# Weight pieces converted in pairs, in place at stride 2, in an attention + SwiGLU kernel on Trainium2

## The chip, the cores and the metric

The kernel runs on one core of one Trainium2 chip. The metric is the time of one execution on the device in microseconds (us); the median of three runs of the kernel before is 1545.31 us. Five engines work side by side and are tied together by semaphores: TensorE (PE, with its weight loads PEld), VectorE (DVE), ScalarE (ACT), GpSimd (POOL) and SyncE (SP, which issues nearly all DMAs). [...]

## The reference, cut to what matters

The inputs arrive as follows: q, k and v have 8 sequences x 12 heads x 448 positions x 64, and the three weight matrices (768 x 1536, 768 x 1536, 1536 x 768) hold 64-bit floats, because they are scaled by a 64-bit number. TensorE multiplies 32-bit floats, so the kernel has to convert the weights on the chip.

```python
q_n, k_n = rmsnorm(q, g_q), rmsnorm(k, g_k)
attn = softmax(q_n @ k_n.T / sqrt(64))        # per sequence and head
x = (attn @ v) -> rows of 768 (12 heads x 64), 3584 rows
xn = rmsnorm(x, rms_g)
g = xn @ w_gate
out = (g * sigmoid(g) * (xn @ w_val)) @ w_out
```

## The kernel before, in words

The work of `safe_scores` goes by pairs of heads, g = 0 to 47, six for each sequence. A pair's attention is a run of score and value products on TensorE with exponentials on ScalarE between them (`score`, `rests`, `values` and `sums` for the first six pairs; `step` and `totals` later). Two halves of each pair's keys and queries are transposed on TensorE by `turn(g, 0)` and `turn(g, 1)`; both write a PSUM tile "tr", and VectorE copies out kT (L550, L552), while ScalarE copies out qT (L549). GpSimd makes the norms of q and k (L514, L515, L520), adds up the exponentials (`es`, L709 and L714), and for two pairs in each sequence scales the last 64 rows (`rest`, L465 to L469).

The first six pairs (g = 0 to 5) and most of the seventh run alone, since there is no x yet to feed the second block. From g = 7 on, the feed-forward work of the previous sequence is cut into items in the list `todo`, and `fill` places some of them between the attention parts of a pair. For the first sequence these are 48 items of `plain` (L1440: six matrix instructions each, 2.25 us), and then 12 items of `project_out` (L1178). From the second sequence on the products use a scheme with fewer multiplications on sums of weight blocks (L1081, L1305, L1373).

All order is written out by hand: `pe(fn)` issues a piece of TensorE work and counts time by one, and `after(n, fn)` puts off work of other engines by n such counts.

The weights come in 72 pieces of 128 x 384 elements: 48 of the gate and value matrices, used by the 48 items of `plain` in that order, and 24 of the output matrix. `convert` is called once per conversion turn (not to be confused with `turn`, the transposes) and handles several pieces at different stages. In conversion turn n it

- adds the two parts of piece n - 5 on GpSimd (L890) into a block of the pool `free_w`, which has NW = 23 blocks;
- joins piece n - 4 on VectorE (`join`, L848 to L850): clamp, shift and mask, and put in sign and exponent bit;
- splits piece n - 3 on ScalarE (`split`, L842 and L843): the absolute value of the high words into a tile `top`, and the scaled low words in place, at a stride of two words, in the raw tile;
- loads piece n on SP (L829) into a raw tile of 64-bit numbers, and stores piece n - 7 in DRAM (`keep`, L878) for the later sequences.

There are 7 raw tiles and 6 tiles for `top`; some of the first 24 pieces borrow a tile of the pool "xs" for `top`. The first conversion turns run in the pairs that are alone: four in g = 0, three in g = 1, three in each of g = 2 to 5, and three in g = 6. So 22 turns are done when the items begin, and after each item `fill` calls `convert` once more, if a block is free (`room`). A block comes free one count after the item that used the piece. After the last turn the tiles of the conversion are handed over to later work, and only then may `ask` begin to load weights for the second sequence.

The lines that the prediction speaks of besides: L566 and L664 are the exponentials; L596 to L598 and L638 are the inversion of a pair's sums and its use; L643 and L644 make and add the squares of x (`rd`, `ss`); L728, L730, L738 and L744 are the root mean square of x and its use (six operations L744 per sequence, put off by 0 to 5 counts); L696 and L699 copy the sums (`rd`) out of PSUM; L1448 is the tanh, L1449 and L1451 are the two products of an item group of `plain`; L530 (`norm_k`) scales the keys, L493 and L457 square them.

Of the kernel before, what the change touches and what calls it, by code (L numbers as in the profile page):

```python
# [8 lines left out]
F32 = mybir.dt.float32  # L9
I32 = mybir.dt.int32  # L10
U32 = mybir.dt.uint32
I64 = mybir.dt.int64
ALU = mybir.AluOpType
ACT = mybir.ActivationFunctionType
# [8 lines left out]
NPAIR = H // 2  # L23
NDC, NFC = DM // 128, DF // 128
HALF = DM // 2
BW = 384
HT = S // 2
# [308 lines left out]
def safe_scores(  # L336
# [20 lines left out]
    nc = tc.nc  # L357

    def pool(name, bufs, **kw):
        return ctx.enter_context(tc.tile_pool(name=name, bufs=bufs, **kw))  # L360

    NW = 23
    const, small = pool("c_const", 1), pool("c_small", 4)
    qk_pool, v_pool, qn_pool, qkT_pool = pool("c_qk", 3), pool("c_v", 3), pool("c_qn", 1), pool("c_qkT", 2)
    e_pool, tmp, y_pool, rest_pool = pool("c_e", 11), pool("c_tmp", 1), pool("c_y", 3), pool("c_rest", 2)
    x_pool, s_pool, slots = pool("c_x", 4), pool("c_xs", 3), pool("c_slots", 1)
    raw_pool, cv_pool, l2_pool = pool("c_raw", 7), pool("c_cv", 6), pool("c_l2", 5)
    scratch = pool("c_dram", 1, space=DRAM)
    ps_s, ps_m, ps_f = pool("c_ps_s", 4, space=PSUM), pool("c_ps_m", 1, space=PSUM), pool("c_ps_f", 3, space=PSUM)

# [3 lines left out]
    st = {}  # L374
# [426 lines left out]
    carried = []  # L801
    free_w = [slots.tile([128, BW], F32, name=f"w{i}") for i in range(NW)]

# [19 lines left out]
    def data(key):  # L823
        return st[key][0][:, 0:BW]

    def load_raw(src):
        raw = raw_pool.tile([128, 2 * BW], I32, name="raw")
        a = src.shape[1]
        nc.sync.dma_start(out=raw.rearrange("p (a n w) -> p a (n w)", a=a, w=2).bitcast(I64), in_=src)  # L829
        return raw  # L830

    def split(raw, n):


        words = raw.rearrange("p (n w) -> p n w", w=2)
        lo, hi = words[:, :, 0], words[:, :, 1]
        if n < 24 and n % 7 > 3:

            top = s_pool.tile([128, 3, HT], I32, name="xs")[:, 0:2].rearrange("p c n -> p (c n)")[:, 0:BW]
        else:  # L840
            top = cv_pool.tile([128, BW], I32, name="top")
        nc.scalar.activation(top.bitcast(F32), hi.bitcast(F32), ACT.Abs)  # L842
        nc.scalar.activation(lo, lo.bitcast(U32), ACT.Copy, scale=2.0**-29)  # L843
        return lo, hi, top

    def join(lo, hi, top):

        nc.vector.tensor_scalar(top.bitcast(F32), top.bitcast(F32), 122879.9921875, 2.0**-15, ALU.min, ALU.max)  # L848
        nc.vector.tensor_scalar(top, top, 3, 0x3FFFFFF8, ALU.logical_shift_left, ALU.bitwise_and)  # L849
        nc.vector.scalar_tensor_tensor(top, hi, -(2**30), top, ALU.bitwise_and, ALU.bitwise_or)  # L850
        return lo, top


    pieces = []
# [11 lines left out]
    room_so = []  # L866
# [13 lines left out]
    def convert():  # L880

        n = turn_of["n"]
        if n >= TURNS or not room(1):
            return False
        turn_of["n"] += 1
        if 0 <= n - 5 < len(pieces):
            key = pieces[n - 5][0]
            st[key] = block()
            lo, top = st.pop(("cv", n - 5))
            nc.gpsimd.tensor_tensor(data(key).bitcast(I32), top, lo, ALU.add)  # L890
        if 0 <= n - 4 < len(pieces):
            st["cv", n - 4] = join(*st.pop(("cv", n - 4)))
        if 0 <= n - 3 < len(pieces):
            st["cv", n - 3] = split(st.pop(("raw", n - 3)), n - 3)
        if n < len(pieces):
            st["raw", n] = load_raw(pieces[n][1])
        if 0 <= n - 7 < len(pieces):
            keep(pieces[n - 7][0])
        if turn_of["n"] == TURNS:

            free_w.extend(cv_pool.tile([128, BW], F32, name="top") for _ in range(4))
            whole = [raw_pool.tile([128, 2 * BW], F32, name="raw") for _ in range(7)]
            room_so.extend(whole[:6])
            homes = [whole[6][:, 0:BW], whole[6][:, BW:]] + [cv_pool.tile([128, BW], F32, name="top")[:, :] for _ in range(2)]
            carried.extend(t.rearrange("p (c n) -> p c n", c=KG) for t in homes)
        return True

# [670 lines left out]
    def turns(n):  # L1578

        for _ in range(n):  # L1580
            convert()
# [18 lines left out]
    for g in range(NG + 1):  # L1600
# [24 lines left out]
        if g <= NPAIR:  # L1625
            pe(lambda: score(g, (0,)))
            squares(g + 2, 0)
            squares(g + 2, 1)
            if g > 1:
                pe(lambda: turn(g + 1, 0))  # L1630
                some_rests(g)
                pe(lambda: turn(g + 1, 1))
            pe(lambda: rests(g))
            pe(lambda: values(g - 1))
            if g == 1:
                pe(lambda: turn(g + 1, 0))
                some_rests(g)
                pe(lambda: turn(g + 1, 1))
            load_v(g + 2)

            turns(1 if g == 1 else 3 if g < NPAIR else 0)
            pe(lambda: sums(g - 1))
            pe(lambda: score(g, (1, 2)))
            turns(2 if g == 1 else 3 if g == NPAIR else 0)
            if g == 2:
                bound()
            if g == NPAIR - 1:
                for half in range(2):
                    norm_k(g + 2, half)
            continue  # L1650
# [90 lines left out]
```

## Time and profile before

| What | Value |
|---|---|
| median of 3 runs | 1545.31 us (1544.56 to 1545.82) |
| profiled execution | 1546.19 us |
| its span in the profile | 1544.4 us |
| busy share of VectorE, ScalarE, GpSimd over the span | 60%, 35%, 48% |
| mean granted TensorE clock | 0.996 of full speed |
| last conversion turn's work on VectorE | ends near 276 us |

The profile is one execution taken by the hardware profiler. Times within it are counted from the start of the span. A group of instructions is named by line of the kernel, engine, operation, and the tiles out<-in; "x63" is how many there are. A wait is named by the instruction that waited and by what released it. A timeline row gives start, length, engine, line and, in brackets, idle time before the instruction and what ended it. The granted clock is the share of TensorE's full clock.

### The profile page before, as it was taken

The numbers are of one execution on the slowest core, as the hardware profiler recorded it, in microseconds if no ns is written. First come the engines' busy times: TensorE is split into PE (matmuls) and PEld (weight loads), VectorE is DVE, ScalarE is ACT, GpSimd is POOL, SyncE is SP. The second block draws the span as 40 slices with busy tenths as digits, with TensorE's granted clock in tenths as the row PEclk, the third lists the DMA queues.
The fourth block names the chain that finished last, engine by engine and source line by source line (L and its number), as shares of the span: only waits on it lengthen the run. The fifth ranks groups of instructions, "written<-read, shape, count | busy, mean of one in ns | idle before, by whom it ended". The sixth has DMA issues, their size and how long they took to land.

```text
span 1544.4 us, 26111 instructions
## 1 busy us (share of the span) xinstructions
PE 1511.2 (98%) x8900; PEld 1187.4 (77%) x8900; DVE 929.8 (60%) x1793; ACT 534.8 (35%) x1241; POOL 736.4 (48%) x718
## 2 busy tenths in 40 slices
PE   8999998999999999999999999999999999999997
PEld 4344444688856888888987888767987889899997
DVE  5788998667754666854457443444458444673464
ACT  6856664333323333234233332424333232101000
POOL 6868887546424354474435652544545731030003
PEclk9999999999999999999999999999999999999998
DMA  7758575776989978886557855584557755577565
GB/s 194 228 153 258 175 228 157 225 229 214 294 274 275 310 253 266 285 250 188 160 163 217 267 176 153 152 275 131 174 155 228 240 160 148 164 256 256 175 194 176
DMA packets 314082, 327.26 MB, mean 212 GB/s; under 512 B 84308, under 2 KB 310868, under 8 KB 313940
## 3 DMA queue, kind: packets, MB, share of 16 engines
q1 hardware_dynamic: 313012, 325.31, 68.1%
q8 instruction: 73, 1.20, 0.3%
q14 instruction: 69, 0.57, 0.1%
q10 hardware_dynamic: 800, 0.20, 0.1%
q0 software_dynamic: 128, 0.00, 0.0%
HBM read 271.62 MB, written 53.77 MB: 211 GB/s over the span
## 4 chain that ended last, share of the span: by engine, by line
PE 83%; DVE 11%; DMA 2%; issue 1%; ACT 1%; POOL 1%; SPq 0%; DVEq 0%; POOLq 0%; ACTq 0%
PE ff L1081 42%; PE ff L1373 10%; PE sc L659 7%; PE av L674 6%; PE ff L1305 5%; PE ff L1440 4%; PE tr L544 2%; PE ff L1178 2%; DVE top L850 1%; DVE top L849 1%; PE den L692 1%; PE den L606 1%; DVE top L848 1%; PE sc L562 1%; DVE l L1248 1%
## 5 line engine op out<-in xcount | busy, mean ns | idle before, releaser
L1081 PE MATMUL ff<-x,w 128*128 128x224 f32 x1686 | 344.4, 354 | 0.0
L1081 PEld LDWEIGHTS ff<-x,w 128*128 128x128 f32 x1686 | 315.2, 190 | 13.2 <-issue 11.3
L1081 PE MATMUL ff<-xs,w 128*128 128x224 f32 x1296 | 265.2, 353 | 2.0 <-DVE w L1003 1.2
L714 POOL TENSOR_TENSOR es<-es,e 128x448 f32<-128x448 f32 x205 | 245.9, 1200 | 13.7
L1081 PEld LDWEIGHTS ff<-xs,w 128*128 128x128 f32 x1296 | 243.9, 190 | 3.4 <-issue 1.5
L659 PE MATMUL sc<-qT,kT 64*64 64x448 f32 x1176 | 233.8, 542 | 5.7 <-ACT e L664 2.9
L674 PE MATMUL av<-e,vt 64*64 64x448 f32 x984 | 194.2, 541 | 0.0
L664 ACT ACTIVATE e<-sc 128x448 f32<-128x448 f32 x294 | 154.4, 547 | 71.4 <-PE sc L659 53.5
L644 POOL TENSOR_TENSOR ss<-ss,rd 128x448 f32<-128x448 f32 x40 | 48.0, 1201 | 218.5 <-ACT rd L643 218.5
L659 PEld LDWEIGHTS sc<-qT,kT 64*64 64x64 f32 x1176 | 79.3, 133 | 87.4 <-issue 61.6
L709 POOL TENSOR_TENSOR es<-e 128x448 f32<-128x448 f32 x41 | 48.2, 1176 | 178.0 <-ACT e L664 178.0
L515 POOL TENSOR_TENSOR rs<-ms,mhalf 128x12 f32<-128x12 f32 (+1 forms) x50 | 115.9, 2319 | 4.2
L1093 DVE TENSOR_TENSOR cc<-ff,u 128x448 f32<-128x448 f32 x84 | 52.3, 623 | 99.6 <-PE ff L1081 99.5
L1440 PE MATMUL ff<-x,w 128*128 128x448 f32 x288 | 111.8, 541 | 0.0
L674 PEld LDWEIGHTS av<-e,vt 64*64 64x64 f32 x984 | 66.2, 133 | 42.4 <-issue 42.4
L1100 ACT ACTIVATE th<-c 128x224 f32<-128x224 f32 x42 | 16.3, 389 | 238.1 <-DVE c L1093 238.1
L1373 PE MATMUL ff<-w,l 128*128 128x192 f32 x500 | 95.6, 329 | 2.8 <-DVE l L1248 2.0
L1440 PEld LDWEIGHTS ff<-x,w 128*128 128x128 f32 x288 | 53.3, 190 | 51.1 <-issue 49.2
L1373 PEld LDWEIGHTS ff<-w,l 128*128 128x128 f32 x500 | 82.6, 190 | 8.1 <-DVE l L1248 3.2
L1345 POOL TENSOR_TENSOR y<-y,c 128x384 f32<-128x384 f32 x10 | 12.2, 1217 | 159.4 <-DVE y L1414 148.0
L1093 DVE TENSOR_TENSOR u<-ff,p 128x448 f32<-128x448 f32 x42 | 26.2, 623 | 84.3 <-PE ff L1081 77.9
L1093 DVE TENSOR_TENSOR u<-ff,u 128x448 f32<-128x448 f32 x42 | 26.1, 623 | 82.6 <-PE ff L1081 82.3
(209 smaller groups left out, 2627.9 us busy)
## 6 DMA issues: line engine op xcount, KB each, us to landing
w<-kept SPq DMA_DIRECT2D x474, 192.0 KB, 3.7
w<-kept_q SPq DMA_DIRECT2D x297, 192.0 KB, 3.8
w<-kept_o SPq DMA_DIRECT2D x132, 192.0 KB, 3.9
kept<-w SPq DMA_DIRECT2D x81, 192.0 KB, 3.9
top<-kept SPq DMA_DIRECT2D x78, 192.0 KB, 3.9
top<-kept_q SPq DMA_DIRECT2D x53, 192.0 KB, 3.2
kept_q<-w SPq DMA_DIRECT2D x52, 192.0 KB, 3.0
qk<-in_q_dram SPq DMA_DIRECT2D x48, 192.0 KB, 3.5
```

What stands on the lines that cost most here:

```text
L515: nc.gpsimd.tensor_tensor(st["rs", g][:, cols], ms, mhalf[:, cols], ALU.pow)
L644: after(m, lambda: (nc.gpsimd.tensor_tensor(ss, ss, rd, ALU.add), st.update({("summed", b): hp})))
L659: nc.tensor.matmul(ps[r, 0:S], lhsT=st["kT", g][r, keys_of(i)], rhs=st["qT", g][r, :], start=True, stop=True)
L664: nc.scalar.activation(e, ps[:, 0:S], ACT.Exp)
L674: nc.tensor.matmul(st["av", g][own(j), 0:S], lhsT=vt, rhs=st["e", g, i][r], start=i == 0, stop=i == PARTS - 1, skip_group_check=True)
L709: nc.gpsimd.tensor_tensor(st["es", g], st["e", g, 0], st["e", g, 1], ALU.add)
L714: nc.gpsimd.tensor_tensor(st["es", g], st["es", g], st["e", g, i], ALU.add)
L1081: nc.tensor.matmul(bank[:, w * HT:(w + 1) * HT], lhsT=wt[:, c * 128:(c + 1) * 128], rhs=x[:, c, :], start=onto is None and w == c == 0, st ...
L1093: nc.vector.tensor_tensor(add[name], ps[:, 0:S], add[other], ALU.add)
L1305: nc.tensor.matmul(ps, lhsT=left_o(b, which, LEFT_O[name], c), rhs=data(("wo", b, name, c)), start=first and c == 0, stop=c == NFP - 1, sk ...
L1373: nc.tensor.matmul(ps, lhsT=a[:, j, :], rhs=data(key)[:, n % 2 * HW:(n % 2 + 1) * HW], start=start and j == 0, stop=j == KG - 1, skip_grou ...
L1440: nc.tensor.matmul(bank[w][:, 0:S], lhsT=data(key)[:, c * 128:(c + 1) * 128], rhs=st["x", 0, half][:, c, :], start=half == c == 0, stop=ha ...
```

## The change

Two pieces are loaded, split and joined together. A raw tile now holds two pieces (4 tiles of double size in place of 7), a tile `low` holds the scaled low words of two pieces (3 tiles of double size in place of 6 tiles `top`), and the pool "xs" is no longer borrowed. The split writes the scaled low words contiguously into `low`, and then the absolute values of the high words into the low words' places in the raw tile, which are two words apart. The join's three operations therefore read and write at a stride of two words, in place, 768 elements each instead of 384. The addition on GpSimd stays one per piece; it reads the stride-2 part from `raw` in place of the former stride-2 low words.

In time, a pair m is loaded in turn 2m, split in turn 2m + 3 (odd turns only), joined in turn 2m + 4 (even turns only), and its two pieces are added in turns 2m + 5 and 2m + 6. In each of the pairs g = 2 to 5, which run alone, four turns are made in place of three, so that 26 are done when the items begin. NW goes from 23 to 21. With 21 pieces added and none used, no block is free then: the item with index 0 is followed by no turn, and the item with index k (1 to 48) by turn 25 + k, where it was turn 22 + k before. In the items of the output product there is again no free block until the second row tile gives blocks back, so that the turns after the items with index 49, 50 and 51 fall out, and the last turns come at the same items as before.

```diff
-    NW = 23
+    NW = 21
...
-    raw_pool, cv_pool, l2_pool = pool("c_raw", 7), pool("c_cv", 6), pool("c_l2", 5)
+    raw_pool, cv_pool, l2_pool = pool("c_raw", 4), pool("c_cv", 3), pool("c_l2", 5)
...
-    def load_raw(src):
-        raw = raw_pool.tile([128, 2 * BW], I32, name="raw")
-        a = src.shape[1]
-        nc.sync.dma_start(out=raw.rearrange("p (a n w) -> p a (n w)", a=a, w=2).bitcast(I64), in_=src)
+    def load_raw(srcs):
+        raw = raw_pool.tile([128, 4 * BW], I32, name="raw")
+        for i, src in enumerate(srcs):
+            part = raw[:, i * 2 * BW:(i + 1) * 2 * BW].rearrange("p (a n w) -> p a (n w)", a=src.shape[1], w=2)
+            nc.sync.dma_start(out=part.bitcast(I64), in_=src)
         return raw

-    def split(raw, n):
+    def split(raw):
         words = raw.rearrange("p (n w) -> p n w", w=2)
         lo, hi = words[:, :, 0], words[:, :, 1]
-        if n < 24 and n % 7 > 3:
-            top = s_pool.tile([128, 3, HT], I32, name="xs")[:, 0:2].rearrange("p c n -> p (c n)")[:, 0:BW]
-        else:
-            top = cv_pool.tile([128, BW], I32, name="top")
-        nc.scalar.activation(top.bitcast(F32), hi.bitcast(F32), ACT.Abs)
-        nc.scalar.activation(lo, lo.bitcast(U32), ACT.Copy, scale=2.0**-29)
-        return lo, hi, top
-
-    def join(lo, hi, top):
+        low = cv_pool.tile([128, 2 * BW], I32, name="low")
+        nc.scalar.activation(low, lo.bitcast(U32), ACT.Copy, scale=2.0**-29)
+        nc.scalar.activation(lo.bitcast(F32), hi.bitcast(F32), ACT.Abs)
+        return lo, hi, low
+
+    def join(top, hi, low):
         nc.vector.tensor_scalar(top.bitcast(F32), top.bitcast(F32), 122879.9921875, 2.0**-15, ALU.min, ALU.max)
         nc.vector.tensor_scalar(top, top, 3, 0x3FFFFFF8, ALU.logical_shift_left, ALU.bitwise_and)
         nc.vector.scalar_tensor_tensor(top, hi, -(2**30), top, ALU.bitwise_and, ALU.bitwise_or)
-        return lo, top
+        return low, top
...
+        m, odd = divmod(n, 2)
         if 0 <= n - 5 < len(pieces):
             key = pieces[n - 5][0]
             st[key] = block()
-            lo, top = st.pop(("cv", n - 5))
-            nc.gpsimd.tensor_tensor(data(key).bitcast(I32), top, lo, ALU.add)
-        if 0 <= n - 4 < len(pieces):
-            st["cv", n - 4] = join(*st.pop(("cv", n - 4)))
-        if 0 <= n - 3 < len(pieces):
-            st["cv", n - 3] = split(st.pop(("raw", n - 3)), n - 3)
-        if n < len(pieces):
-            st["raw", n] = load_raw(pieces[n][1])
+            pair, at = divmod(n - 5, 2)
+            lo, top = st["cv", pair]
+            cols = slice(at * BW, (at + 1) * BW)
+            nc.gpsimd.tensor_tensor(data(key).bitcast(I32), top[:, cols], lo[:, cols], ALU.add)
+            if at:
+                st.pop(("cv", pair))
+        if odd and ("raw", m - 1) in st:
+            st["cv", m - 1] = split(st.pop(("raw", m - 1)))
+        if not odd and ("cv", m - 2) in st:
+            st["cv", m - 2] = join(*st["cv", m - 2])
+        if not odd and n < len(pieces):
+            st["raw", m] = load_raw([src for _, src in pieces[n:n + 2]])
...
-            turns(1 if g == 1 else 3 if g < NPAIR else 0)
+            turns(1 if g == 1 else 4 if g < NPAIR else 0)
```

The lines left out of the diff hand the four raw and three low tiles over to later work after the last turn; together with the 21 blocks they give 27 blocks again, as 23 and 4 did before.

## The prediction

> **What bounds the kernel now.** I read the page first, for the share of each engine:
>
> ```profile
> PE 1511.2 (98%) x8900; PEld 1187.4 (77%) x8900; DVE 929.8 (60%) x1793; ACT 534.8 (35%) x1241; POOL 736.4 (48%) x718
> ```
>
> TensorE is busy 98% of the span, so nothing can be gained beyond its waits. Next come the waits of TensorE in the first 330 us, the only part in which weights are converted (engine, line, what it waited for: us in total, times, longest):
>
> ```profile
> PE tr L544 <- DVE kT L550: 3.2, 1, 3.2
> PE sc L659 <- ACT e L664: 2.9, 1, 2.9
> PE sc L659 <- DVE x L744: 2.7, 1, 2.7
> ```
>
> Three waits make 8.8 us; all the other waits of that list are 1.5 us or less. In order of time they end at 199.35 us (on ACT), 240.53 (on kT) and 261.14 (on x). The busy time in stretches says which engine is late there (columns: stretch, length, then busy of PE, PEld, DVE, ACT, POOL, granted clock, DMA):
>
> ```profile
> 180.00:200.00 20.00, 17.07 (x78) 8.02 (x80) 19.52 (x31) 9.96 (x25) 18.79 (x19) 1.00 0.36 101
> ...
> 220.00:240.00 20.00, 17.36 (x103) 8.24 (x101) 19.38 (x27) 13.40 (x31) 13.72 (x13) 1.00 0.85 248
> 240.00:260.00 20.00, 17.87 (x73) 9.35 (x73) 19.52 (x34) 7.96 (x17) 14.64 (x14) 1.00 0.55 172
> 260.00:280.00 20.00, 18.86 (x80) 10.32 (x81) 9.82 (x18) 7.28 (x18) 12.62 (x12) 0.91 0.20 65
> ```
>
> VectorE is busy 97% around all three; GpSimd is nearly full around the first alone. After the third the granted clock falls (0.57 from 262 to 266 us), which is another 0.43 x 4 = 1.7 us. From 280 us on TensorE hardly waits, so what is saved before that should reach the end. The groups of VectorE up to 330 us show what fills it, and the times of the single line show why (min/median/max ns):
>
> ```profile
> L850 DVE SCALAR_TENSOR_TENSOR top<-raw,top 128x384 int32<-128x384 int32 x63 | 51.6, 818 | 2.2
> L849 DVE TENSOR_SCALAR top<-top 128x384 int32<-128x384 int32 x63 | 45.9, 728 | 2.2
> L848 DVE TENSOR_SCALAR top<-top 128x384 f32<-128x384 f32 x63 | 39.1, 621 | 4.5 <-ACT top L842 4.5
> ```
> ```profile
> L848 DVE TENSOR_SCALAR top<-top x63: 342/525/1283, 26.7 to 275.0; 128x384 f32<-128x384 f32 x63
> ```
>
> With the nine that use xs, the three operations take 603 + 708 + 803 = 2.11 us per piece on average (sums of both groups over 72). Undisturbed they take 0.342 + 0.359 + 0.557 = 1.26 us (minima of the three lines). The other 0.86 us, 0.29 per instruction, is waiting beside GpSimd: in the timeline long ones end when a GpSimd operation ends. The 240.53 wait in the timeline of VectorE, and the 199.35 one on GpSimd:
>
> ```profile
> 236.88 0.86 DVE L848 TENSOR_SCALAR top<-top 128x384 f32<-128x384 f32 x1
> 237.78 1.17 DVE L849 TENSOR_SCALAR top<-top 128x384 int32<-128x384 int32 x1
> 238.98 1.37 DVE L850 SCALAR_TENSOR_TENSOR top<-raw,top 128x384 int32<-128x384 int32 x1
> 240.27 0.21 DVE L550 COPY kT<-tr 128x64 f32<-128x64 f32 x1
> ```
> ```profile
> 193.90 1.64 POOL L466 TENSOR_TENSOR msr<-msr,mhalf 128x6 f32<-128x6 f32 x1
> 195.61 0.96 POOL L469 TENSOR_TENSOR rest<-rest,msr 128x384 f32<-128x384 f32 x1
> 196.53 6.95 POOL L890 TENSOR_TENSOR w<-top,raw 128x384 int32<-128x384 int32 x6
> ```
> ```profile
> 197.88 0.55 ACT L842 ACTIVATE top<-raw 128x384 f32<-128x384 f32 x1 [6.03 <-POOL w L890]
> ```
>
> The small kT copy stands behind three joins; the exponentials of the pair stand behind a split that waits 6.03 us for the first of six late additions, which gives its top buffer back.
>
> [...]
>
> **The change part by part.**
> *Joins.* Two pieces now cost three instructions of 768 instead of six of 384. [...] Three waits beside GpSimd instead of six: 0.86. So 2.92 us per pair of pieces against 4.23. [...] I take 2.92: the read at stride 2 and ScalarE's write were free. From the start of the interleaved part (97 us) before joins 54 pieces, 54 x 2.11 = 114 us; after joins 25 pairs, 73 us. 41 us leave an engine that had 10.5 us idle from 100 to 260.
> *Splits.* Four activations start 0.45 us apart (1.80 us). Two of 768 take 563 + 384 x 0.8 = 0.87 us each (slope from 421 ns for 256 and 523 for 384, L457), the second waiting for the first: 1.75 us. Nothing is gained, but it comes in one lump.
> *Low buffers.* Three pair buffers: a split now waits for an addition issued three turns earlier, not four. Splits fall on odd turns. The last turns of the item groups ending at 168, 193 and 220 us are odd (49, 57, 65), so there ScalarE waits one more addition (1.05) and holds 0.87 more before the exponentials: 1.9 us. At 168 the timeline shows 0.16 us of slack on the den banks and rd copies that wait for TensorE until 169.07: cost 0.8. At 199 GpSimd should be some 1 us earlier, with less waiting beside VectorE: cost 0.9. At 220 ScalarE had 1.6 us of idle time: 0.1, left out.
> *Joins before kT.* Pairs 11 and 12 have a pair join right ahead of L550. At 213.12 it ran 0.46 us ahead of its reader; a full join beside GpSimd (1.18 + 1.18 + 1.38 + 0.8 = 4.5 us) against the 3.75 there costs 0.3 us with that slack and 0.7 without it; I take 0.7. At 240 two pair joins replace three single ones, but the last 1.9 us of joins before 225.4 (turn 65 has none) go: L550 at about 238.3 instead of 240.27; gain 2.2 of 3.2.
> *x at 261.* L744's six operations stood between joins from 251.9 to 261. Item 48 now has an odd turn, and items 49 and 50 find no free block, so no join stands between them and they run from 248 on: gain 2.7, next late are the exponentials, which have no split ahead. The clock loss of 1.7 us: I count 1.0, since two waits of the same length had none.
> *At 92 us.* Before, three joins (84.2 to 91.3) stood ahead of L728, whose root made TensorE wait 0.7 us; after, one. Gain 0.7.
> *Four turns.* In pairs 2 to 5 VectorE has two pair joins (5.8 us) for three pieces (6.3): nothing. GpSimd gets a fourth addition (0.98 us). Its queue then delays ss, rms and qn: following it from 40.5 us, idle 0.57 and 0.22 absorbs some, and qn of pair 7 ends at 74.3 instead of 72.3, needed at 73.73. That 0.6 is covered by norm_k on ScalarE, for which TensorE waits until 75.2 anyway; without that cover it costs 0.6. Queued behind on SP: the second load of a pair comes a turn earlier, raw is given back two turns ahead as before: nothing.
> *Blocks.* 21 are full when pair 7 starts; each later addition takes the block of the item just computed. GpSimd runs behind TensorE there and the piece is needed 20 items later: nothing; up to 1 us if it were ahead.
>
> Sum: -0.7 + 0.8 + 0.9 + 0.7 - 2.2 - 2.7 - 1.0 = -4.2 us. The profiled execution took 1546.19 us (span 1544.4 and 1.8 around it), so 1542.0 in its terms; the median of the three runs is 0.9 lower: 1541.1.
>
> **The rivals.**
> *Given back at the group ends.* Splits in lumps and three low buffers put ScalarE late by the full 1.9 at 199, the clock still falls, and 240 gains 1.0: -0.7 + 0.8 + 1.9 + 0.7 - 1.0 - 2.7 = -1.0, or 1544.3. For it: GpSimd is 94% busy from 180 to 200, and its work is not less. Against: two of the three waits are VectorE's.
> [...]
> *Little of it moves.* All waits go, with the clock: -0.7 - 8.8 - 1.7 = -11.2, or 1534: bounds the gain.
>
> **How the numbers follow.** A measurement of this kernel tells about 0.2% from no change, 3.1 us: faster is below 1542.2, slower above 1548.4. Chances: the forecast 0.52 (1536 to 1543, a tenth of it inside the band), given back 0.22 (1542 to 1549), slow writes 0.21 (1549 to 1560), all waits gone 0.05. That makes faster 0.49, same 0.26, slower 0.25. The range is 1536 to 1554: below it half of the last case, above it half of the slow writes.
>
> **What would show it.** In the profile after: the joins at about 0.54 us undisturbed for the two one-source operations and 0.96 for the third (1.47 would say slow writes); VectorE under 80% from 100 to 260 us; no wait of TensorE on x near 261 and one near 1 us on kT near 240; a wait on e near 195 to 200 of 3 to 4 us. I am wrong if new waits on ScalarE stand at the head of pairs, if kT waits grow, or if waits appear after 280 us.

## The result, and the profile after

The changed kernel is slower: 1558.93 us (1557.65 to 1560.03, four runs) against 1545.13 us (1544.56 to 1545.82, four runs) of the kernel before; ratio 1.0089, 95% interval 1.0071 to 1.0106. The forecast was 1541.1 us with a range up to 1554. The profiled execution took 1560.03 us, its span 1558.2 us. The joins, which the change was to make cheaper, came out as forecast; two other places lost far more than they gave.

The page's busy line of the changed kernel shows that VectorE has less work, and that the kernel takes more time:

```profile
PE 1516.8 (97%) x8900; PEld 1188.5 (76%) x8900; DVE 887.3 (57%) x1685; ACT 533.1 (34%) x1169; POOL 744.4 (48%) x718
```

VectorE is busy 42.5 us less than before (929.8), GpSimd 8 us more with the same 718 instructions. The joins by line of the changed kernel, L845 to L847 (all of the 36 pairs of pieces; min/median/max ns):

```profile
L845 DVE TENSOR_SCALAR raw<-raw x36: 547/730/1529, 27.0 to 271.7; 128x768 f32<-128x768 f32 x36
```
```profile
L846 DVE TENSOR_SCALAR raw<-raw x36: 560/567/1452, 27.6 to 273.1; 128x768 int32<-128x768 int32 x36
```
```profile
L847 DVE SCALAR_TENSOR_TENSOR raw<-raw x36: 958/961/1777, 28.2 to 273.7; 128x768 int32<-128x768 int32 x36
```

The minima are 0.55, 0.56 and 0.96 us, the forecast of an undisturbed join (0.54, 0.56, 0.96). So no price of stride 2 in place shows on VectorE. Where, then, did the time go? The waits of TensorE in the first 330 us answer (engine, line, what it waited for: us in total, times, longest):

```profile
PE sc L659 <- ACT e L664: 4.3, 1, 4.3
PE sc L659 <- ACT rd L699: 3.3, 2, 2.5
PE av L576 <- DVE x L638: 2.7, 2, 2.1
PE tr L544 <- DMA qk<-in_k_dram: 2.1, 1, 2.1
PE tr L544 <- DVE kT L550: 2.0, 1, 2.0
PE av L576 <- DVE kT L550: 2.0, 1, 2.0
```

The wait on x at 261 us is gone and the one on kT at the transposes is 2.0 instead of 3.2. New are the waits of L576 (`av`, the values of the pairs that run alone). L659 now waits for ScalarE three times, at the heads of pairs 10 to 12, 7.6 us in all, where it waited once before, 2.9 us. The stretches (length, busy of PE, PEld, DVE, ACT, POOL, granted clock, DMA) show that VectorE is no longer what is full (52 to 79%, forecast under 80%):

```profile
180.00:200.00 20.00, 18.09 (x79) 8.59 (x80) 13.41 (x21) 14.81 (x29) 13.59 (x13) 0.91 0.67 206
200.00:220.00 20.00, 15.66 (x77) 6.27 (x76) 10.38 (x13) 7.43 (x12) 18.61 (x17) 0.83 0.50 148
220.00:240.00 20.00, 19.97 (x73) 9.77 (x75) 13.21 (x17) 10.74 (x19) 14.85 (x14) 1.00 0.56 183
240.00:260.00 20.00, 17.20 (x92) 8.58 (x85) 15.72 (x23) 13.18 (x27) 15.45 (x13) 1.00 0.79 252
260.00:280.00 20.00, 20.00 (x102) 10.10 (x101) 12.96 (x17) 9.19 (x16) 15.03 (x14) 1.00 0.21 64
```

To place the loss I compared the start of the first transpose (L544) of each pair with that of the same pair before. Nearly all of it arises in two stretches, and one stretch gains. The table gives, for all kernels of this study, the us lost since the stretch's beginning; the stretches are named by the times of the kernel before. Each row comes from one profiled execution, so that some tenths mean nothing. That of e7 was 4.6 us under the kernel's median time, those of e6, e8 and e14 were 3.4, 2.0 and 1.7 us under it; the others lie within 1.1 us of it.

| kernel | lone pairs, 31 to 104 | heads, 104 to 234 | 234 to 271 | 271 to 301 |
|---|---|---|---|---|
| changed kernel | +8.6 | +9.5 | -5.8 | 0.0 |
| e1 pairs, three turns | +0.2 | +6.6 | -1.7 | 0.0 |
| e2 singles, four turns | +17.1 | -0.1 | -1.8 | 0.0 |
| e3 even last turns | +7.9 | +7.7 | -6.2 | +1.2 |
| e4 less GpSimd | +6.3 | +8.6 | -4.1 | 0.0 |
| e5 three turns, four low tiles | +0.2 | -2.3 | -6.4 | +2.9 |
| e6 three turns, split by piece | +4.4 | +13.4 | -2.2 | 0.0 |
| e7 singles, less slack | 0.0 | +0.8 | -2.4 | 0.0 |
| e8 by piece, more low tiles | +6.1 | +16.0 | -6.8 | +2.7 |
| e9 four turns, four low tiles | +7.8 | +2.9 | -4.2 | +2.9 |
| e10 less VectorE | +5.7 | +8.2 | -4.5 | 0.0 |
| e11 less ScalarE | +7.7 | +9.8 | -5.8 | 0.0 |
| e12 two turns, four low tiles | -0.9 | -0.9 | -3.8 | +4.4 |
| e13 one pair with four turns | +5.2 | +1.6 | -4.4 | +2.8 |
| e14 less of both | +2.0 | +8.2 | -5.8 | 0.0 |
| e15 three turns, two slots fewer | +0.3 | +6.6 | -6.2 | +2.9 |

Outside these stretches the kernels differ by up to 1.4 us at the start (the first loads of q and k) and 2.3 us after 301.

A part of some rows is a lower clock of TensorE and not waiting itself. In the lone pairs of the changed kernel the granted clock was 1.00, but in the same stretch it was 0.50 for 17.1 us in e2, for 6.8 us in e8 and e11, and for 3.4 us in e10 and e13. In the changed kernel the pairs of products L659 start 0.75 to 0.80 us apart at a clock of 0.50 (from 181.9 and 214.0 us on), and 0.37 to 0.38 us apart at 1.00 (from 177.7 us on). So by my estimate half of TensorE's busy time at this clock is lost, that is 8.5, 2.9, 3.0, 1.7 and 1.7 us of their losses.

**The lone pairs.** The timeline of the changed kernel around 41 us (start, length, engine, line):

```profile
40.21 0.86 DVE L845 TENSOR_SCALAR raw<-raw 128x768 f32<-128x768 f32 x1
...
41.11 0.75 DVE L846 TENSOR_SCALAR raw<-raw 128x768 int32<-128x768 int32 x1
41.41 4.97 POOL L890 TENSOR_TENSOR w<-raw,low 128x384 int32<-128x384 int32 x4
41.90 1.67 DVE L847 SCALAR_TENSOR_TENSOR raw<-raw 128x768 int32<-128x768 int32 x1
...
43.48 0.64 DVE L596 STREAM_TRANSPOSE rd<-den 128x448 f32<-128x448 f32 x1
44.15 0.24 DVE L597 RECIPROCAL few<-rd 128x14 f32<-128x14 f32 x1
44.43 0.65 DVE L598 STREAM_TRANSPOSE rd<-few 128x448 f32<-128x448 f32 x1
...
45.11 0.62 DVE L638 TENSOR_TENSOR x<-av,rd 128x448 f32<-128x448 f32 x1
...
45.88 0.97 PE L576 MATMUL av<-e,vr 64*64 64x448 f32 x4 [2.08 <-DVE x L638]
```

The first values of the next pair need the bank that L638 empties, and L638 stands behind both joins. Rows between are left out at the dots. The same place before:

```profile
40.24 0.74 DVE L850 SCALAR_TENSOR_TENSOR xs<-raw,xs 128x384 int32<-128x384 int32 x1
...
42.53 0.62 DVE L638 TENSOR_TENSOR x<-av,rd 128x448 f32<-128x448 f32 x1
...
43.30 0.97 PE L576 MATMUL av<-e,vr 64*64 64x448 f32 x4
```

L638 ended 0.15 us before its reader started: there was no slack. Three single joins ran there from 36.76 to 40.98, 4.2 us. Two pair joins run from 38.14 to 43.57, 5.4 us, and begin 1.4 us later; 0.52 us of that is waiting for the split of both pieces (L840), and the kT copy ahead of the joins (L552) ends 0.8 us later than before. GpSimd makes four additions in a row and has only one break, of 0.47 us, from 37.25 to 82.9 us.

**The heads.** The timeline of ScalarE, GpSimd and TensorE at the head of pair 11:

```profile
209.66 6.21 POOL L890 TENSOR_TENSOR w<-raw,low 128x384 int32<-128x384 int32 x6
211.68 0.90 ACT L839 ACTIVATE low<-raw 128x768 int32<-128x768 uint32 x1 [5.53 <-POOL w L890]
212.61 0.90 ACT L840 ACTIVATE raw<-raw 128x768 f32<-128x768 f32 x1
213.41 1.83 ACT L664 ACTIVATE e<-sc 128x448 f32<-128x448 f32 x4
...
213.99 1.01 PE L659 MATMUL sc<-qT,kT 64*64 64x448 f32 x2 [4.34 <-ACT e L664]
```

The scores of the exponentials were done at 209.6 us, but the exponentials stand behind a split on ScalarE, and the split stands idle for 5.53 us until GpSimd's late additions give a low tile back. TensorE's granted clock falls to 0.50 while it waits, 0.2 us before the wait ends at 181.91 us and 1.5 us before the one that ends at 213.99, and stays there for 3.41 and 6.83 us (third column from the end; the first line is the head of pair 10, the second that of pair 11):

```profile
181.72:185.13 3.41, 3.22 (x20) 1.22 (x24) 3.07 (x7) 2.10 (x5) 0.80 (x1) 0.50 1.02 325
212.44:219.27 6.83, 5.28 (x25) 1.80 (x26) 4.43 (x3) 4.35 (x10) 6.57 (x6) 0.50 0.84 244
```

TensorE is busy for 3.22 and 5.28 us of these stretches; at half the clock that is 1.6 and 2.6 us more. It waits 2.50, 4.34 and 0.78 us at the three heads, 7.6 us against 2.9 before. So 4.7 + 1.6 + 2.6 = 8.9 of the 9.5 us are found.

### The profile page after: what moved, and what is told of

It is laid out like the page before. It is cut to its first block, busy times and chain, and to the rows that moved or that the text cites. A ratio compares the mean times of both kernels' runs of the same rounds, so it can differ in the third digit from the quotient of the medians.

```text
span 1558.2 us, 25940 instructions
## 1 busy us (share of the span) xinstructions
PE 1516.8 (97%) x8900; PEld 1188.5 (76%) x8900; DVE 887.3 (57%) x1685; ACT 533.1 (34%) x1169; POOL 744.4 (48%) x718
## 4 chain that ended last, share of the span: by engine, by line
PE 85%; DVE 6%; DMA 2%; POOL 2%; ACT 2%; issue 2%; SPq 1%; POOLq 0%; DVEq 0%; ACTq 0%
PE ff L1084 43%; PE ff L1376 10%; PE sc L659 8%; PE av L674 6%; PE ff L1443 6%; PE ff L1308 5%; PE ff L1181 2%; PE tr L544 2%; PE den L692 1%; DVE l L1251 1%; DMA qk<-in_k_dram 1%; POOL w L890 1%; DVE xs L761 1%; POOL rs L515 0%; PE av L589 0%
## 5 line engine op out<-in xcount | busy, mean ns | idle before, releaser
L1084 PE MATMUL ff<-x,w 128*128 128x224 f32 x1506 | 309.5, 354 | 0.0
L1084 PEld LDWEIGHTS ff<-x,w 128*128 128x128 f32 x1506 | 281.8, 190 | 11.1 <-issue 9.9
L1084 PE MATMUL ff<-xs,w 128*128 128x224 f32 x1194 | 245.8, 353 | 2.2 <-DVE w L1006 1.2
L659 PE MATMUL sc<-qT,kT 64*64 64x448 f32 x1176 | 236.2, 547 | 7.6 <-ACT e L664 4.3
L1084 PEld LDWEIGHTS ff<-xs,w 128*128 128x128 f32 x1194 | 224.7, 190 | 3.6 <-issue 1.5
L659 PEld LDWEIGHTS sc<-qT,kT 64*64 64x64 f32 x1176 | 79.6, 134 | 94.4 <-issue 62.9
L1084 PE MATMUL ff<-x,low 128*128 128x224 f32 x510 | 108.3, 354 | 0.0
L1084 PEld LDWEIGHTS ff<-x,low 128*128 128x128 f32 x510 | 95.1, 190 | 5.6 <-issue 4.9
L1443 PEld LDWEIGHTS ff<-x,w 128*128 128x128 f32 x288 | 53.5, 191 | 51.8 <-issue 50.6
L1376 PE MATMUL ff<-w,l 128*128 128x192 f32 x444 | 87.1, 329 | 2.7 <-DVE l L1251 2.0
L890 POOL TENSOR_TENSOR w<-raw,low 128x384 int32<-128x384 int32 x72 | 80.1, 1133 | 19.2 <-PE ff L1443 8.2
```

Of the source, the lines that this page charges most:

```text
L659: nc.tensor.matmul(ps[r, 0:S], lhsT=st["kT", g][r, keys_of(i)], rhs=st["qT", g][r, :], start=True, stop=True)
L890: nc.gpsimd.tensor_tensor(data(key).bitcast(I32), top[:, cols], lo[:, cols], ALU.add)
L1084: nc.tensor.matmul(bank[:, w * HT:(w + 1) * HT], lhsT=wt[:, c * 128:(c + 1) * 128], rhs=x[:, c, :], start=onto is None and w == c == 0, st ...
L1376: nc.tensor.matmul(ps, lhsT=a[:, j, :], rhs=data(key)[:, n % 2 * HW:(n % 2 + 1) * HW], start=start and j == 0, stop=j == KG - 1, skip_grou ...
L1443: nc.tensor.matmul(bank[w][:, 0:S], lhsT=data(key)[:, c * 128:(c + 1) * 128], rhs=st["x", 0, half][:, c, :], start=half == c == 0, stop=ha ...
```

## The experiments

Two questions follow. In the lone pairs, does the fourth turn cost the 8.6 us, whatever the pairing, or do the lumps of the pairing cost them? At the heads, is it the odd last turns, which the prediction had counted, too few low tiles (theory S from e5 on), or the lump of two splits ahead of the exponentials, whoever frees the tile (theory L)?

### e1: pairs, three turns

```diff
-            turns(1 if g == 1 else 4 if g < NPAIR else 0)
+            turns(1 if g == 1 else 3 if g < NPAIR else 0)
```

Expected:

> The changed kernel with three turns instead of four in pairs 2 to 5 (pairs of pieces kept). Theory A (the fourth addition fills GpSimd in the lone pairs, buffers come back late; and splits on odd last turns hold ScalarE at the heads of pairs): turns are then 22 + k after item k, the last turns 46, 54, 62 are even, so both losses go (8.9 us up to the first item, some 9 at the heads near 180 and 214) and most of the gain of 5.9 stays: about 1541. Rival B (the lumps of two pieces themselves delay x and kT in the lone pairs, whatever the number of turns): the first item starts at about 103 us instead of 97, total 1547 to 1550.

Measured: 1551.99 us, ratio 1.0048 (1.0031 to 1.0065). The lone pairs lose 0.2 us: the fourth turn is the whole 8.6, and with three turns the lumps of the pairing cost nothing there. The heads still lose 6.6 us although the last turns ahead of pairs 10 to 12 are now even, so odd ones are at most a part.

### e2: the kernel before, with four turns

```diff
-            turns(1 if g == 1 else 3 if g < NPAIR else 0)
+            turns(1 if g == 1 else 4 if g < NPAIR else 0)
```

> The kernel before with four turns in pairs 2 to 5 and nothing else changed. Theory A: GpSimd is as full as in the changed kernel, the first item starts 4 to 8 us later than 97 us; with single pieces and more buffers the heads of pairs stay as before: 1550 to 1553. Rival B: three single joins become four, no lump, first item at 98 to 99 us: about 1546.

Measured: 1560.57 us, ratio 1.0105 (1.0085 to 1.0125). Piece by piece the fourth turn costs 17.1 us in the lone pairs, twice as much as in pairs; there TensorE waits four times, 10.4 us in all, for the exponentials L566, and by the estimate above half of the 17.1 us, 8.5, is its lower clock. So the pairing makes a fourth turn no dearer; the difference is as large as the loss by the clock. The heads lose nothing, though all of this kernel runs later and with a fourth turn: their loss belongs to the pairing.

### e3: even last turns, four turns kept

One block is kept from `free_w` until the last turn, so that each item is followed by a turn of the other parity:

```diff
+    late_w = [free_w.pop()]
...
+            free_w.extend(late_w)
```

> The changed kernel with one of the 21 blocks held back until the last turn, so that every turn of the items comes one number later and the last turns before the heads of pairs 10, 11 and 12 are 48, 56 and 64 (even: no split there, no join ahead of kT in pairs 11 and 12). Theory A on the heads: the lone pairs lose the same 8.9 us, the two waits of 2.65 and 4.5 us and the low clock behind them go: 1549 to 1551. Rival C (ScalarE is late there because GpSimd is late from the lone pairs on, whatever the parity): no change, 1557 to 1560.

Measured: 1556.87 us, ratio 1.0073 (1.0056 to 1.009). The heads lose 7.7 instead of 9.5 us. So the odd last turns cost something, but only 1.8 us of the 9.5.

### e4: less GpSimd in the lone pairs

```diff
+            if b == 1:
+                return
...
+            if b == 1:
+                nc.gpsimd.tensor_scalar(rest, rest, 0.125, None, ALU.mult)
+                return
```

> The changed kernel with four turns, but the root mean square of the last 64 rows of the second sequence is left out: its add, power and scaling on GpSimd are replaced by one multiplication with a constant, which takes some 2 to 2.5 us off GpSimd in each of pairs 3 and 4 and changes the values of that sequence. Theory A: the lone pairs lose 3 to 5 us less, total 1554 to 1556. Rival B: GpSimd is not what delays the lone pairs, the first item starts at 105 us or later, total 1558 to 1559.

Measured: 1556.29 us, ratio 1.0072 (1.0056 to 1.0089). 2.3 of the 8.6 us come back by 104 us: GpSimd counts there, but is not the whole.

### e5: three turns and a fourth low tile

```diff
-    NW = 21
+    NW = 19
...
-    raw_pool, cv_pool, l2_pool = pool("c_raw", 4), pool("c_cv", 3), pool("c_l2", 5)
+    raw_pool, cv_pool, l2_pool = pool("c_raw", 4), pool("c_cv", 4), pool("c_l2", 5)
...
-            ends = [cv_pool.tile([128, 2 * BW], F32, name="low") for _ in range(3)]
+            ends = [cv_pool.tile([128, 2 * BW], F32, name="low") for _ in range(4)]
...
+            turns(1 if g == 1 else 3 if g < NPAIR else 0)
```

> Three turns between the lone pairs as in e1, and four low tiles of a pair instead of three (two slots fewer, so that it fits). e1 lost 6.6 us against the kernel before from 104 to 234 us, at the heads of pairs 10 to 12. Theory S (the low tiles come back too late: a split takes one that the additions freed three turns ago, before it was four): the fourth tile gives five turns, ScalarE's waits for GpSimd's additions ahead of the Copy go from some 30 us to under 15, the heads lose under 2.5 us, and the time is about 1547.5. Theory L (two pieces' splits in a row, 1.85 us, stand ahead of the exps of the head, whoever frees the tile): as e1, about 1552, heads 5 to 7 us.

Measured: 1540.89 us (1540.3 to 1541.84, ten runs) against 1545.49 us of the kernel before on the same chip, ratio 0.9974 (0.9965 to 0.9984): faster than both kernels. The heads gain 2.3 us where e1 lost 6.6. The lump is as large as in e1 (both splits in a row, 0.93 us each) and costs nothing here, where the last turns ahead of the heads are even: as the cause of e1's loss L falls, and S holds. What the splits waited for, from the groups of the first 330 us (the last part of the line is idle time before, by what ended it), in the changed kernel:

```profile
L839 ACT ACTIVATE low<-raw 128x768 int32<-128x768 uint32 x36 | 33.0, 917 | 41.2 <-POOL w L890 34.6 <-DMA raw<-in_moe_w_val_dram 6.6
```

in e1:

```profile
L839 ACT ACTIVATE low<-raw 128x768 int32<-128x768 uint32 x36 | 33.3, 925 | 35.8 <-POOL w L890 34.4 <-DMA raw<-in_moe_w_gate_dram 1.4
```

and in e5:

```profile
L839 ACT ACTIVATE low<-raw 128x768 int32<-128x768 uint32 x36 | 33.3, 925 | 13.6 <-DMA raw<-in_moe_w_out_dram 12.0 <-DMA raw<-in_moe_w_gate_dram 1.4 <-DMA raw<-in_moe_w_val_dram 0.3
```

34.4 us of waiting for GpSimd's additions become none. Unexpected was a loss of 2.9 us from 271 to 301 us, where output products (L1181) wait for additions (waits of TensorE in the first 330 us):

```profile
PE ff L1181 <- POOL w L890: 1.7, 3, 0.7
```

### e6 and e8: each piece split in a turn of its own

```diff
-        if odd and ("raw", m - 1) in st:
-            st["cv", m - 1] = split(st.pop(("raw", m - 1)))
+        if ("raw", m - 1) in st:
+            lows = st["cv", m - 1][2] if odd else []
+            st["cv", m - 1] = split(st["raw", m - 1], odd, lows)
+            if odd:
+                st.pop(("raw", m - 1))
```

`split` works on one half of the raw tile into a low tile of 384; three turns; six such tiles in e6, eight in e8 (two slots fewer there).

> Three turns between the lone pairs as in e1; each piece is split in a turn of its own (two operations of 384, the first piece one turn earlier, the second as before), into six low tiles of one piece each; the join stays one for two pieces. A low tile is taken three turns after its last reading ended, as in e1. Theory L (the lump of two splits ahead of the exps): the heads lose 2 us or less instead of 6.6, time about 1547.5. Theory S (the low tiles' slack): as e1, 1552, or a little later by the fixed cost of two more ScalarE operations a pair (4 of some 0.55 us instead of 2 of 0.92).

> e6 with eight low tiles of one piece instead of six (two slots fewer): lump and slack both as good as, or better than, in the kernel before; only the paired join and the even or odd end of the turns remain of the change. Theory S and theory L both give heads that lose under 1.5 us, and about 1545 to 1547 where the wait behind the joins at 266 us stays as in e1 (3.1 us). If the heads still lose 5 us or more, neither is the cause, and it is the paired join itself or GpSimd's lateness behind it (theory J), time about 1552.

Measured: 1565.26 us, ratio 1.0134 (1.0117 to 1.0151), and 1566.87 us, ratio 1.0152 (1.013 to 1.0174). Neither theory expected this. To keep three turns of slack, the first piece is split one turn earlier, two turns after its load. In e8 the wait for additions is gone, and the raw data takes its place:

```profile
L839 ACT ACTIVATE low<-raw 128x384 int32<-128x384 uint32 x72 | 39.8, 553 | 41.4 <-DMA raw<-in_moe_w_out_dram 23.7 <-DMA raw<-in_moe_w_gate_dram 12.2 <-DMA raw<-in_moe_w_val_dram 5.5
```

41.4 us of idle time before the splits, as much as in the changed kernel, and 16.0 us lost at the heads. So these two are no test of the lump; e8 shows that the heads also lose where the split's late partner is the load and not the addition.

### e7: the kernel before, with a turn less of slack

```diff
-    NW = 23
+    NW = 24
...
-    raw_pool, cv_pool, l2_pool = pool("c_raw", 7), pool("c_cv", 6), pool("c_l2", 5)
+    raw_pool, cv_pool, l2_pool = pool("c_raw", 7), pool("c_cv", 5), pool("c_l2", 5)
...
-        if n < 24 and n % 7 > 3:
-            top = s_pool.tile([128, 3, HT], I32, name="xs")[:, 0:2].rearrange("p c n -> p (c n)")[:, 0:BW]
-        else:
-            top = cv_pool.tile([128, BW], I32, name="top")
+        top = cv_pool.tile([128, BW], I32, name="top")
```

> The kernel before, one piece at a time, with five tiles for the high words instead of six and without the three borrowed from xs: a tile is taken three turns after its last reading, as in the changed kernel, not four. Theory S: it loses at the heads what e1 lost there, 5 to 7 us, time about 1551. Theory L: it loses nothing at the heads, or up to 1 us, time about 1545 to 1546.

Measured: 1547.27 us (1542.63 to 1549.92), ratio 1.0009 (1.0001 to 1.0016). In the profile the heads lose 0.8 us, not 5 to 7, and the splits wait 21.7 us for additions, against 16.7 in the kernel before and 34.4 in e1. This speaks against theory S as worded there, that three turns of slack are too few in themselves. It doesn't refute it: the profiled execution was the fastest of all 17, 4.6 us under the median, and no trace shows where the median one loses these 4.6 us. At the heads they would make 5.4 us, as S expected. The reading that three turns are too few only where a tile of two pieces comes free with the second addition fits e5 and this profile, but it is argued, not shown.

### e9: four turns, four low tiles

The edit of e5 without its last line.

> The changed kernel with its four turns, and four low tiles of a pair instead of three (two slots fewer). With three turns the fourth tile took the time from 1552.0 to 1540.9. Theory W (the fourth turn's own work is too much for the lone pairs' engines): the lone pairs lose 7 to 9 us again by 104 us, the heads behave as in e5, and the time is about 1549.5. Theory S reaches back (the fourth turn is late in the lone pairs because its split waits for a low tile, as at the heads): the lone pairs lose under 3 us and the time is 1541 to 1543.5.

Measured: 1555.52 us, ratio 1.0069 (1.0052 to 1.0086). The lone pairs lose 7.8 us: the fourth turn's cost is its work (W), not the low tile. The heads lose 2.9, less than the changed kernel's 9.5, but 5.2 more than e5; that was not expected, and e13 takes it up.

### e10, e11: less VectorE, less ScalarE in the lone pairs

The first edit is in the join (e10), the second in the split (e11), where the join's first operation then reads the high words themselves. The lines that choose the first twelve pairs of pieces are left out.

```diff
+        if clamp:
+            nc.vector.tensor_scalar(top.bitcast(F32), top.bitcast(F32), 122879.9921875, 2.0**-15, ALU.min, ALU.max)
```
```diff
+        if not alone:
+            nc.scalar.activation(lo.bitcast(F32), hi.bitcast(F32), ACT.Abs)
```

> The changed kernel (four turns, three low tiles), where the joins of the first twelve pairs of pieces leave out their clamp (the first of three VectorE operations, 0.55 to 0.85 us each); it leaves out the guard against values outside the format's range. Read at 104 us, where the lone pairs end and the changed kernel had lost 8.9 us. Theory V (joins in a row on VectorE keep the copies that free the bank of PSUM): 3 to 5 us of it come back, the loss is 4 to 6, the time about 1555. Theory G (GpSimd, busy without a break from 37 to 83 us, sets the pace of these pairs): at most 1 us comes back, the time about 1558.

> The changed kernel, where the splits of the first twelve pairs of pieces leave out their Abs (0.93 us of ScalarE each), and their joins clamp the signed high words instead; negative weights of these pieces are lost. Read at 104 us. Theory A (ScalarE: exps of the pair behind the splits): 3 to 5 us of the 8.9 come back, time about 1555. Theory G: GpSimd is as full as before, but its additions start earlier where the join was waiting for the Abs, so 0 to 1.5 us, time about 1558.

Measured: 1555.61 us (1550.78 to 1557.2), ratio 1.0058 (1.0038 to 1.0079), and 1555.82 us (1550.24 to 1557.95), ratio 1.0065 (1.0046 to 1.0084). At 104 us the losses are 5.7 and 7.7 instead of 8.6, so 2.9 us come back without VectorE's clamps and 0.9 without ScalarE's absolute values. But both kernels ran part of the lone pairs at half the clock (the first line is e10, the second e11):

```profile
77.28:80.69 3.41, 3.41 (x13) 1.76 (x15) 2.65 (x5) 3.41 (x11) 2.43 (x2) 0.50 0.97 316
77.20:84.03 6.83, 6.07 (x22) 2.43 (x23) 4.07 (x9) 5.12 (x14) 6.66 (x9) 0.50 0.77 238
```

The changed kernel did not. With half of TensorE's busy time there added, 1.7 and 3.0 us, my estimate of what is saved is 4.6 us for VectorE and 3.9 for ScalarE. So VectorE's work is on the path of the lone pairs, within what theory V expected. Whether ScalarE's is too stays open: the 0.9 us alone speak against it, the estimate for it. The executions of both kernels also lie further apart than most, by 6.4 and 7.7 us, and one profile of each can't settle it.

### e14: less of GpSimd and of VectorE together

The edits of e4 and e10 together.

> The changed kernel with the edits of e4 and e10 together: in the lone pairs the root of the rests is left out on GpSimd (a constant stands in its place), and the joins of the first twelve pairs of pieces leave out their clamp. Read at 104 us; the changed kernel loses 8.6 us from 31 to 104 us, e4 6.3, e10 5.7. If the costs lie one behind the other in a turn (theory O: the pace is GpSimd's additions and norms after VectorE's joins, each on the path), the gains add: 8.6 - 2.3 - 2.9 = 3.4 us or less. If each relief only uncovers another limit (theory M), they don't add: 5 to 5.7 us.

Measured: 1554.53 us, ratio 1.0066 (1.0049 to 1.0082). The loss at 104 us is 2.0 us, so 6.6 us come back, where the two alone gave 2.3 + 2.9, or 2.3 + 4.6 by the estimate without e10's low clock; e4 and e14 ran the lone pairs at 1.00. So in the profiles the gains add, as they do if both engines' work lies one behind the other on the path of the lone pairs (O). The whole times say less: the medians of e4, e10 and e14 are 2.6, 3.3 and 4.4 us under that of the changed kernel.

### e12: two turns, four low tiles

```diff
+            turns(1 if g == 1 else 2 if g < NPAIR else 0)
```

> Four low tiles of a pair as in e5, and two turns between the lone pairs instead of three; the turns left out are made later, up to the beginning of the first block's products. Theory W (every turn there costs, the fourth most): the lone pairs gain up to 1 us on e5, where TensorE still stood 1.0 us at 60 us; the later conversion then costs about as much (a weight that comes late at 270 us, where e5 stood 2.2 us already), so 1540 to 1543. If the pieces come late at 250 to 300 us the time is over 1544. A gain of more than 1 us on e5 is expected by neither theory.

Measured: 1543.99 us (1542.24 to 1546.64), ratio 0.9994 (0.9988 to 1.0001). The lone pairs gain another 1.1 us on e5; later stretches give 5.5 back (heads -0.9 for -2.3, 234 to 271 -3.8 for -6.4, then +4.4 for +2.9). Three turns are best of the three numbers tried.

### e13: a fourth turn after one pair only

```diff
+            turns(1 if g == 1 else (4 if g == 2 else 3) if g < NPAIR else 0)
```

with the four low tiles of e5.

> e5 (four low tiles) with a fourth turn after pair 2 alone and three after pairs 3 to 5, so that one pair pays for it and the last turns ahead of the heads fall on odd numbers, as in the changed kernel. Theory E (each lone pair pays for its own fourth turn): some 2 us lost by 104 us against e5, not 7.6 as in e9. Theory P (an odd last turn leaves a whole split of two pieces ahead of the exps): with four low tiles the head of pair 10 loses 4 us at 179 us as in e9, and the time is about 1540.9 + 2 + 4 = 1547. If the parity is nothing in itself (what e9 lost there came from the lone pairs' lateness), 1543.

Measured: 1552.46 us, ratio 1.0045 (1.0028 to 1.0061), 5 us more than expected. The pair with four turns pays 2.1 us by 53 us, 3.0 against e5, where E has some 2, but by 104 us 5.2 are lost: the later lone pairs lose 2.9 more with three turns, whose even and odd turns, and so whose joins, now fall the other way round; 1.7 us of it is the lower clock (0.50 from 92.3 to 95.7 us). At the heads 1.6 us are lost against e5's gain of 2.3. That fits P, but since the lone pairs came out 5.2 us late here too, the parity isn't separated from their lateness. At the head of pair 10 TensorE waits 2.4 us; the split ahead of it now waits for its load:

```profile
175.42 0.93 ACT L839 ACTIVATE low<-raw 128x768 int32<-128x768 uint32 x1 [6.57 <-DMA raw<-in_moe_w_gate_dram]
176.38 0.91 ACT L840 ACTIVATE raw<-raw 128x768 f32<-128x768 f32 x1
177.31 1.06 ACT L699 COPY rd<-den 64x448 f32<-64x448 f32 x2
```

This wait of 6.57 us for a load explains the place, not why the load was late; that stays open.

### e15: e1 with two slots fewer

```diff
-    NW = 21
+    NW = 19
```

with three turns and three low tiles.

> e1 (three turns, three low tiles) with two slots fewer and nothing in their place: what the fourth low tile was paid with. From 271 to 301 us the kernels with 19 slots lost 2.8 us (e5, e9) and those with 21 or 23 none. Theory N (the slots): the same 2.8 us here, and otherwise e1, so about 1554.5. If 1552 and nothing lost there, the loss comes from the fourth tile's later raw loads or something else in e5, and not from the slots. A gain against e1 would mean that the slots, not the tile, made e5 faster; no theory expects that.

Measured: 1550.39 us, ratio 1.0038 (1.0024 to 1.0052). From 271 to 301 us it loses 2.9 us and at the heads 6.6, as e1: the 2.9 us are the price of the two slots (N), which have no part in the fourth tile's gain at the heads. From 234 to 271 it gains 6.2 us, where e1 gained 1.7; in e1 TensorE still waited 3.0 us on x (L744), here no longer. No theory expected that the time falls below e1's; a reading that wasn't tested is the prediction's own one for 261 us: without free blocks no join comes between L744's operations.

## Why the prediction was wrong

- *Joins: right.* The means are 850 + 902 + 1190 ns = 2.94 us a pair, forecast 2.92. That forecast held 2.06 us without waits, and that of kT at 213 us held 0.8 us for the larger size; no run of the kernel before shows what a one-source operation of 768 elements takes. In place of the two, the minima gave 0.547 + 0.560 + 0.958 = 2.07 us, 0.81 more than the 1.26 of a single piece. The waiting beside GpSimd stayed (maxima of 1.5 to 1.8 us): of the 108 operations 48 took over 15% more than the minimum of their line, and in each of them a GpSimd operation ended, 0.42 to 0.43 us (L845, L846) or 0.82 us (L847) before the join's operation did; in the kernel before it was 100 of 216, and 0.21 to 0.22 us (L848, L849) or 0.41 to 0.42 us (L850). The rival of slow stride-2 writes named the right side for a wrong cause: no run shows its price of 1.47 us for each operation, with which the minima would lie far above 547, 560 and 958 ns. That "the read at stride 2 and ScalarE's write were free" rests on rows of the kernel before: L850 reads the high words at a stride of two words in 557 ns at the least, where L1003, with two sources of 384 adjacent ones, took 541; ScalarE's L843 writes at that stride in 563 ns on average, against 557 of L842.
- *Splits: right in size* (0.92 + 0.93 = 1.85 us, forecast 1.75), and e5 shows that the lump is harmless where the last turns are even. With odd ones (e9, e13) its part isn't separated from the late tiles and loads.
- *Four turns: wrong, and the larger of the two failures.* "In pairs 2 to 5 VectorE has two pair joins (5.8 us) for three pieces (6.3): nothing." Measured: +8.6 us (e1 takes all of it back). The 6.3 was the mean of the whole conversion, 3 x 2.11, with 0.86 us of waiting beside GpSimd in each. In the stage itself, in the place shown, three single joins took 4.2 us and two pair joins 5.4, and they started 1.4 us later. The other half, "that 0.6 is covered", followed GpSimd's queue to qn alone. With less work on GpSimd, on VectorE or on both, 2.3, 2.9 and 6.6 us of the 8.6 come back in the profiles (e4, e10, e14). The reader L638, whose slack was 0.15 us, stood in no part of the working.
- *Low buffers: mechanism right, size wrong.* Named were the heads and the late addition; forecast 0.8 + 0.9 and 0.7 for kT at 213 us, 2.4 in all, measured 9.5; the wait on kT there did not come. It priced one more addition (1.05 us) and one more operation. In fact the splits' waiting for additions doubles, from 16.7 us to 34.6 in the first 330 us, since GpSimd makes up to six additions in a row and gives a tile back only with the second one of a pair. One wait of 6.03 us stood in the kernel before too, at one head; now three heads stand behind such waits. TensorE's clock falls as well (0.50 for 3.41 and 6.83 us), which by the estimate above costs 1.6 and 2.6 us; the sum held nothing of this for new waits. Odd last turns are a fifth of the 9.5 us (e3), too few low tiles most: a fourth tile brings 9.5 down to 2.9 with four turns (e9), and e1's 6.6 to a gain of 2.3 with three (e5).
- *kT at 240 and x at 261: right, the sum in part by luck.* -2.2 - 2.7 - 1.0 = -5.9 forecast, -5.8 measured from 234 to 271 us. The wait on x went, as forecast. That on kT stayed at 2.0 us, a gain of 1.2 and not 2.2; the clock, 1.00 from 260 to 280, gave back the whole 1.7 us and not 1.0.
- *At 92 us: wrong, small.* The wait for the root (L730) stays at 0.8 us; the 0.7 did not come.
- *Blocks: "nothing", right* for the changed kernel with 21 (0.0 from 271 to 301); with 19 it is 2.9 us (e15).

What stays open is why e9 and e13, with odd last turns and four low tiles, are 5.2 and 3.9 us behind e5 at the heads (from 165 to 215 us their splits still wait, e9's 7.4 us for additions and 6.9 for loads, e13's 14.3 for loads), and how the lone pairs' 8.6 us divide among GpSimd, VectorE and ScalarE.

## What to carry to other kernels

An average over a stage-mixed row is no price for one stage: before a step is booked at nothing, take the operation's times in the very window, and look for the reader with the least slack behind it on the same engine. When work is batched by two, ask which partner frees its buffers last, and how late that partner runs: here one more buffer of a pair (paid with 2.9 us of slots) turned a loss of 0.5% into a gain of 0.26%.

## What the runs showed of the hardware

One-source VectorE operations of 32-bit words, reading and writing in place at a stride of two words, ran 768 elements per partition in 547 and 560 ns (minima of L845 and L846 in the changed kernel), against 342 and 359 ns for 384 adjacent ones (L848 and L849 on `top` in the kernel before): 205 and 201 ns for 384 more elements, 0.53 ns each. The two-source one took 958 ns (L847) against 557 (L850), 1.04 ns for each further element.

The granted clock of TensorE was 0.50 for 6.8 us, from 212.4 us on, around the end of a wait of 4.3 us, and for 3.4 us, from 181.7 us on, around the end of one of 2.5. In the kernel before it fell (0.57 from 262 to 266 us) at a wait of 2.7 us, but not at those of 2.9 and 3.2 us, so the length of a wait alone doesn't decide it.
